# Score bursts across the pairs of a batch, and two PSUM banks left to the MLP

## The chip, the cores and the metric

The kernel runs on one core of a Trainium2 chip. The metric is the device time of one execution in microseconds, as a median of runs. The engines are TensorE (PE, with its weight loads as PEld), VectorE (DVE), ScalarE (ACT), GpSimd (POOL) and SyncE (SP, which here only issues DMAs).

## The reference

Eight batches of eight heads with 576 tokens of 64 dimensions go through causal attention with 16 beacon keys ahead of the keys; the beacons are seen by every query. The result, as 4608 tokens of 512, goes through an MLP with a squared ReLU.

```python
scores = scale * np.matmul(q, k_all.transpose(0, 1, 3, 2))   # k_all: 16 beacons, then 576 keys
scores = np.where(causal, -1000000000.0, scores)
...
a /= a.sum(-1, keepdims=True) + 1e-09
attn = np.matmul(a, v_all)
...
h = x @ w_in            # 4608 x 512 by 512 x 2048
r = np.maximum(h, 0.0)
g = r * r
return (g @ w_out).astype(np.float32)
```

## The kernel before, in words

**Attention.** Work is done by pairs of heads: four pairs a batch, 32 in all, numbered p. Scores are made transposed, with 128 keys on the partitions and the queries along the columns. The two heads of a pair lie in partitions 0 to 63 and 64 to 127 of kT and qT, so that a score matmul (L584) has 64 rows and the two heads' matmuls use the two halves of the PE array. A pair of batches 1 to 7 has four *pieces* (WHOLE): columns 496, 464, 336 + 80 and 208 + 80 of each head. A piece goes into two PSUM banks next to each other, one a head. ScalarE takes its exponential into a tile pt (L597); when all four pieces are there, VectorE sets the causal triangle with a minimum (L607, L611). Then PE makes the product with the values (L627, "av", 30 matmuls of 65 columns, where the 65th column sums the weights), and VectorE divides (L642, L643) into xn. Batches 0 and 1 are transposed for the MLP on PE (L691), the later ones by DMAs from SP's queue. Batch 0 is cut into two phases with pieces of their own (SPLIT).

**MLP.** It goes by nine chunks of 512 tokens. First layer ("s1", L755): for each of 16 blocks of hidden units four matmuls of 512 columns into one bank, then a ReLU on ScalarE (L772) or VectorE (L774), then for each two blocks a squaring on VectorE (L781). Second layer ("s2", L792): for each 128 tokens 16 matmuls into one bank, copied out by ScalarE (L355) and stored.

**The order of the instructions** is planned by the class Order while the kernel is built. Each entry (an Op) has an engine, an estimated duration, a priority (lower goes first), dependencies, and a claim on a pool. Order.run steps through time with these estimates and gives each free engine the ready entry of lowest priority; what it finds is each engine's instruction order on the chip, where semaphores do the waiting. Its rules around the change:

- PSUM is a pool of eight banks (Banks). A request for 2 means an even bank and the next one. Classes have limits on the banks that they may use at once: "strip" (scores) 4, "av" 4, "mlp" 4, "tp" (transposes) 2.
- If a ready entry with a request of more than one part finds no place (`short`), entries of a higher priority number are held to `floors`: the MLP may then not go above 2 banks.
- The score entries of a pair have a `gate` (L555): they wait until the MLP has progressed by a set share for each pair (6.2 us of MLP work). A gated entry is still taken when PE has nothing else.
- Estimates: L310 and L313 for ScalarE and VectorE, LAT (L93) for signals, DRAIN (0.096) on PE for each change between entries of mode "rows" (scores), "columns" and "full".

add_pair claims one of four tiles pt and calls add_phase. There a *burst* is one entry "qk" on PE: all matmuls of two pieces of one pair (of one piece in batch 0), with one claim of 2 banks for each piece. Each piece's exponential is an entry of its own and gives its two banks back. After them add_phase adds the mask, the value product (priority lower than the scores') and the division. All chunks of the MLP have priorities behind every score entry.

Of the kernel before, what the change touches and what calls it, by code (L numbers as in the profile page):

```python
# [88 lines left out]
class Order:  # L89
# [3 lines left out]
    LAT = {"PE": 0.2, "ACT": 0.15, "DVE": 0.12, "POOL": 0.15, "SP": 0.1, "-": 0.0}  # L93
    DRAIN = 0.096

    def __init__(self, pools, limits, floors):
        self.pools = dict(pools)
        self.limits = dict(limits)
        self.floors = dict(floors)
        self.inuse = {k: 0 for k in limits}  # L100
        self.ops = []
        self.progress = 0.0
# [7 lines left out]
    def run(self):  # L110
# [24 lines left out]
        mode = None  # L135
        while events:
            now = events[0][0]
            while events and events[0][0] <= now + 1e-9:
                _, _, kind, op = heapq.heappop(events)
                if kind == "done":  # L140
                    for u in op.users:
                        u.left -= 1
                        if u.left == 0:
                            release(u)
                elif kind == "give":
                    owner, k = op.give if isinstance(op.give, tuple) else (op.give, None)
                    pool, cls, wants = owner.take
                    for i in range(len(wants)) if k is None else [k]:
                        self.pools[pool].give(wants[i], owner.held[i])
                        if cls in self.inuse:  # L150
                            self.inuse[cls] -= wants[i]
            again = True
            while again:
                again = False
                for e in engines:
                    if free[e] > now + 1e-9:
                        continue
                    best = None
                    fallback = None
                    short = min((op.prio for op in avail[e] if op.take and len(op.take[2]) > 1  # L160
                                 and (op.gate is None or op.gate(self))
                                 and self.pools[op.take[0]].find(op.take[2]) is None), default=None)
                    for op in avail[e]:
                        if any(free[x] <= now + 1e-9 for x in op.engs[:op.engs.index(e)]):
                            continue
                        if op.take:
                            pool, cls, wants = op.take
                            if self.pools[pool].find(wants) is None:
                                continue
                            if cls in self.limits:  # L170
                                most = self.limits[cls]
                                if short is not None and op.prio > short:
                                    most = min(most, self.floors.get(cls, most))
                                if self.inuse[cls] + sum(wants) > most:
                                    continue
                        if op.gate is not None and not op.gate(self):
                            if fallback is None or op.prio < fallback.prio:
                                fallback = op
                            continue
                        if op.dma and len(lanes[e]) >= 8 and lanes[e][-8] > now + 1e-9:  # L180
                            continue
                        if best is None or op.prio < best.prio:
                            best = op
                    if best is None:
                        best = fallback
                    if best is None:
                        continue
                    op = best
                    started.add(id(op))
                    for u in op.followers:  # L190
                        u.left -= 1
                        if u.left == 0:
                            release(u)
                    for ee in op.engs:
                        avail[ee].remove(op)
                    if op.take:
                        pool, cls, wants = op.take
                        op.held = self.pools[pool].take(wants)
                        if cls in self.inuse:
                            self.inuse[cls] += sum(wants)  # L200
                    dur = op.dur[e] if isinstance(op.dur, dict) else op.dur
                    if e == "PE":
                        dur += self.DRAIN * (mode not in (None, op.mode))
                        mode = op.mode
                    end = now + dur
                    free[e] = end
                    self.progress += op.pe_time
                    issued.append((op, e, now))
                    seq += 1
                    heapq.heappush(events, (end, seq, "free", op))  # L210
                    if op.dma:
                        dma_free = max(dma_free, now + 0.6) + op.dma
                        seen = max(end, dma_free + 1.6)
                        lanes[e].append(seen)
                        seq += 1
                        heapq.heappush(events, (seen, seq, "free", op))
                    else:
                        seen = end + self.LAT[e]
                    seq += 1
                    heapq.heappush(events, (seen, seq, "done", op))  # L220
                    if op.give is not None:
                        seq += 1
                        heapq.heappush(events, (seen, seq, "give", op))
                    again = True
# [12 lines left out]
def kernel(  # L237
# [11 lines left out]
    nc = tc.nc  # L249
    B, H, S, D = q.shape  # L250
    Nb = beacon_k.shape[2]
    HP = H // 2
# [57 lines left out]
    def act(n):  # L310
        return 0.066 + n / 1200.0
# [6 lines left out]
    def wait_for(later, first):  # L318
# [2 lines left out]

    order = Order(
        pools={"ps": Banks(), "stg": Slots(NSTG), "pt": Slots(NPT)},
        limits={"strip": 4, "av": 4, "mlp": 4, "tp": 2},
        floors={"mlp": 2},
    )
    order.wait_for = wait_for
    add = order.add
# [211 lines left out]
                 (0, 2): 1232, (0, 3): 1360, (1, 2): 1536, (1, 3): 1664, (1, 4): 1792, (0, 4): 1872}),  # L540
    ]
    NSPLIT = 1

    def phases(b):
        return SPLIT if b < NSPLIT else WHOLE

# [4 lines left out]
    def add_pair(b, pr):  # L551
# [11 lines left out]
            qk_deps = trans[b, "k"] + trans[b, "q"]  # L563
        take_pt = add(f"pt{p}", "-", 0.0, None, prio=100.0 * p, deps=qk_deps, take=("pt", "pt", [1]), gate=gate)
        av_ops[p] = []
        for n, ph in enumerate(phases(b)):
            add_phase(b, pr, p, n, ph, take_pt, qk_deps, gate)

    def add_phase(b, pr, p, n, ph, take_pt, qk_deps, gate):
        base = 100.0 * p + 1000.0 * n  # L570
        exps = []
        twos = 2 if b >= NSPLIT else 1
        for i in range(0, len(ph.pieces), twos):
            group = ph.pieces[i:i + twos]
            cols = sum(t1 - t0 for mms, _, _ in group for _, t0, t1, _ in mms)
            box = {}

            def emit_qk(e, group=group, box=box):
                for k, (mms, _, _) in enumerate(group):
                    st = pair(box["qk"], k)  # L580
                    for c, t0, t1, at in mms:
                        for hj in range(2):
                            hp = slice(64 * hj, 64 * hj + 64)
                            nc.tensor.matmul(  # L584
                                st[:, hj, at:at + t1 - t0],
                                kT[b % 2][hp, pr, 128 * c:128 * c + 128],
                                qT[b % 2][hp, pr, t0:t1],
                                start=True, stop=True,
                            )

            qk = add(f"qk{p}.{n}.{i}", "PE", cols / 2400.0, emit_qk, prio=base + i,
                     deps=qk_deps + [take_pt], take=("ps", "strip", [2] * len(group)), gate=gate, mode="rows")
            box["qk"] = qk
            qk_ops[p].append(qk)
            for k, (_, off, width) in enumerate(group):
                def emit_exp(e, off=off, width=width, k=k, box=box):
                    nc.scalar.activation(pt[take_pt.held[0]][:, :, off:off + width],  # L597
                                         pair(box["qk"], k)[:, :, 0:width], AF.Exp, bias=0.0, scale=scale)

                exps.append(add(f"exp{p}.{n}.{i + k}", "ACT", act(2 * width), emit_exp, prio=base + i + k,  # L600
                                deps=[qk], give=(qk, k)))

        def emit_mask(e):
            P = pt[take_pt.held[0]]
            at, step, m0, m = ph.diag
# [226 lines left out]
    for b in range(B):  # L832
# [22 lines left out]
            add_weights()  # L855
        if b == 1:
            add_weights_out()
        for pr in range(HP):
            add_pair(b, pr)
        if b < NXPE:  # L860
            add_xt_pe(b)
        else:
# [41 lines left out]
```

## Time and profile before

| | us |
|---|---|
| median of 3 runs | 348.35 (348.26 to 348.68) |
| the profiled execution | 349.44 |
| its span from first to last instruction | 347.7 |
| PE busy in it | 331.8 |
| ScalarE busy | 202.3 |
| VectorE busy | 150.2 |
| GpSimd busy | 84.8 |

The terms of the prediction are worked out on the profiled execution. A busy time is that in which at least one instruction of the engine was running; matmuls are pipelined, so the length of one row (379 ns for 512 columns) is longer than the distance from one to the next. Rows of the timeline and of the chain have the start, the length, the engine, the tiles and the line, and xN where N instructions in a row are merged. A few per cent of the matmul records are missing: a merged row of the second layer may say x15 where the code has 16.

### The profile page before, as it was taken

To read this page: it belongs to the slowest core of one execution; us is meant where nothing else is said; L and a number is where in the kernel's file an instruction comes from. 1 tells how busy PE (TensorE), PEld (TensorE's weight loads), DVE (VectorE), ACT (ScalarE), POOL (GpSimd) and SP (SyncE) were. 2 spreads that over 40 slices of the span, in tenths; PEclk is the share of its full clock that TensorE was granted. 3 is DMA by queue.
4 is the path that set the end of the run, shared out by engine and by line. 5 is a ranking of instruction groups with operands and counts; after the bars stand their busy time and mean duration, and the time that the engine had idled before them with its cause. 6 is when DMAs were issued, how large, how long until landed. Compare 5 with 4: busy or idle time off the path is not lost.

```text
span 347.7 us, 7270 instructions
## 1 busy us (share of the span) xinstructions
PE 331.8 (95%) x2944; PEld 177.7 (51%) x2980; DVE 150.2 (43%) x306; ACT 202.3 (58%) x311; POOL 84.8 (24%) x132
## 2 busy tenths in 40 slices
PE   3799999999999999999999999999999999999995
PEld 2568765554544444544446874454454444444442
DVE  5466683448722464256523772266323302301300
ACT  2678893497854775577655765677536416614611
POOL 8273740357242046105520452000000000000000
PEclk9999999999999999999999999999999999999999
DMA  7989999899978999899986999750014011011002
GB/s 99 188 126 205 221 206 215 192 248 213 201 150 194 208 207 204 130 237 201 238 173 135 215 242 227 120 139 2 3 60 128 2 60 60 2 60 60 3 15 105
DMA packets 137010, 49.50 MB, mean 142 GB/s; under 512 B 123344, under 2 KB 132048, under 8 KB 136976
## 3 DMA queue, kind: packets, MB, share of 16 engines
q1 hardware_dynamic: 127472, 40.09, 55.7%
q0 software_dynamic: 9504, 8.95, 16.0%
q8 instruction: 23, 0.38, 0.5%
q14 instruction: 11, 0.09, 0.1%
HBM read 37.22 MB, written 9.44 MB: 134 GB/s over the span
## 4 chain that ended last, share of the span: by engine, by line
PE 92%; DMA 3%; issue 2%; ACT 1%; DVE 1%; POOL 0%; SPq 0%; ACTq 0%; POOLq 0%
PE ps L755 36%; PE ps L792 36%; PE ps L627 9%; PE ps L584 8%; DMA stg<-in_v_dram 2%; PE ps L480 1%; DMA qk_area<-in_q_dram 1%; PE ps L691 1%; ACT pt L597 1%; DVE pt L607 1%; PE ps L476 0%; DVE g L774 0%; POOL vb L357 0%; ACT osb L355 0%; POOL qk_area L463 0%
## 5 line engine op out<-in xcount | busy, mean ns | idle before, releaser
L755 PE MATMUL ps<-xT,w_in 128*128 128x512 bf16 (+3 forms) x688 | 132.8, 340 | 1.2 <-issue 0.5
L792 PE MATMUL ps<-w_out,g 128*128 128x512 bf16 x556 | 127.8, 379 | 2.0 <-issue 1.4
L597 ACT ACTIVATE pt<-ps 128x832 bf16<-128x832 f32 (+4 forms) x128 | 103.8, 869 | 43.9 <-PE ps L584 41.9
L755 PEld LDWEIGHTS <-w_in 128*128 128x128 bf16 x704 | 65.1, 98 | 56.1 <-issue 5.3
L772 ACT ACTIVATE g<-ps 128x512 bf16<-128x512 f32 (+2 forms) x128 | 71.7, 560 | 36.0 <-PE ps L755 34.7
L792 PEld LDWEIGHTS <-g 128*128 128x128 bf16 x576 | 53.9, 98 | 66.7 <-issue 4.8
L781 DVE TENSOR_TENSOR g<-g 128x1024 bf16<-128x1024 bf16 (+2 forms) x80 | 51.8, 649 | 71.8 <-ACT g L772 71.0
L355 ACT COPY osb<-ps 128x512 f32<-128x512 f32 x36 | 21.1, 587 | 47.4 <-PE ps L792 41.5
L357 POOL CAST vb<-stg 128x512 bf16<-128x512 f32 (+1 forms) x38 | 26.8, 714 | 78.2 <-DMA stg<-in_v_dram 74.0
L607 DVE TENSOR_TENSOR pt<-pt,tri 128x1024 bf16<-128x1024 bf16 (+1 forms) x36 | 24.8, 693 | 45.4 <-ACT pt L597 44.0
L357 POOL CAST qk_area<-stg 128x512 bf16<-128x512 f32 (+2 forms) x50 | 33.2, 676 | 28.2 <-DMA stg<-in_k_dram 14.8
L627 PEld LDWEIGHTS <-pt 128*128 128x128 bf16 (+1 forms) x960 | 34.9, 100 | 8.6 <-issue 1.6
L627 PE MATMUL ps<-vb,pt 128*128 128x65 bf16 (+1 forms) x960 | 36.8, 197 | 1.0 <-POOL vb L357 0.5
L584 PE MATMUL ps<-qT,kT 64*128 64x80 bf16 (+6 forms) x400 | 36.4, 291 | 1.0 <-ACT pt L597 1.0
L774 DVE TENSOR_SCALAR g<-ps 128x512 bf16<-128x512 f32 (+2 forms) x32 | 19.6, 612 | 19.3 <-PE ps L755 18.9
L643 DVE TENSOR_TENSOR xn<-ps,rcp 128x640 bf16<-128x640 f32 (+2 forms) x36 | 27.0, 751 | 1.3
L584 PEld LDWEIGHTS <-kT 64*128 64x128 bf16 x400 | 13.0, 97 | 21.1 <-issue 17.5
L642 DVE RECIPROCAL rcp<-ps 128x10 f32<-128x10 f32 (+2 forms) x36 | 7.6, 211 | 32.4 <-PE ps L627 32.2
L355 ACT COPY qT<-ps 128x576 bf16<-128x576 bf16 x12 | 7.8, 651 | 11.2 <-PE ps L480 11.2
L480 PE MATMUL ps<-ident,qk_area 96*64 96x96 bf16 x288 | 11.1, 233 | 2.7 <-DMA qk_area<-in_q_dram 1.2
L357 DVE COPY kT<-ps 128x16 bf16<-128x16 bf16 (+1 forms) x24 | 9.9, 453 | 5.2 <-PE ps L480 5.0
L480 PEld LDWEIGHTS <-qk_area 96*64 96x64 bf16 x288 | 8.6, 126 | 4.0 <-DMA qk_area<-in_q_dram 2.1
(31 smaller groups left out, 57.2 us busy)
## 6 DMA issues: line engine op xcount, KB each, us to landing
out_dram<-osb SPq DMA_DIRECT2D x17, 512.0 KB, 3.2
stg<-in_v_dram SPq DMA_DIRECT2D x21, 256.0 KB, 5.7
stg<-in_q_dram SPq DMA_DIRECT2D x20, 256.0 KB, 4.9
stg<-in_k_dram SPq DMA_DIRECT2D x15, 256.0 KB, 5.1
w_in<-in_moe_w_in_dram POOLq DMA_DIRECT2D x4, 512.0 KB, 8.7
w_out<-in_moe_w_out_dram POOLq DMA_DIRECT2D x4, 512.0 KB, 10.9
stg<-in_v_dram SPq DMA_DIRECT2D x7, 224.0 KB, 5.2
qk_area<-in_k_dram POOLq DMA_DIRECT2D x4, 288.0 KB, 12.4
```

Source lines behind the costliest of these rows:

```text
L355: nc.scalar.copy(dst, src)
L357: eng[e].tensor_copy(dst, src)
L480: nc.tensor.transpose(pp[64 * hj:64 * hj + 64, half, at + u * NP:at + (u + 1) * NP], t[b % 2][:, 2 * pr + hj, u, :], ident[0:NP, 0:NP])
L584: nc.tensor.matmul(st[:, hj, at:at + t1 - t0], kT[b % 2][hp, pr, 128 * c:128 * c + 128], qT[b % 2][hp, pr, t0:t1], start=True, stop=True,)
L597: nc.scalar.activation(pt[take_pt.held[0]][:, :, off:off + width], pair(box["qk"], k)[:, :, 0:width], AF.Exp, bias=0.0, scale=scale)
L607: nc.vector.tensor_tensor(out=d, in0=d, in1=tri[:, m0:m0 + m, :][:, None].to_broadcast([128, 2, m, 128]), op=ALU.min)
L627: nc.tensor.matmul(a[:, hj, (t - tl[0]) * (D + 1):(t - tl[0] + 1) * (D + 1)], P[0:rr, hj, o:o + 128], vb[b % 2][0:rr, c, h, :], start=(c = ...
L643: nc.vector.tensor_tensor(out=xn[b % 2].rearrange("p t (h d) -> p h t d", d=D)[:, 2 * pr:2 * pr + 2, tl[0]:tl[0] + nt], in0=a[:, :, :, 0:D ...
L755: nc.tensor.matmul(h[:, lo - spans[0][0]:hi - spans[0][0]], w_in_sb[:, mc, ft * 128:(ft + 1) * 128], xT[:, mc, lo % RING:lo % RING + hi - lo],
L772: nc.scalar.activation(dst, h, AF.Relu, bias=0.0, scale=1.0)
L781: nc.vector.tensor_tensor(out=d, in0=d, in1=d, op=ALU.mult)
L792: nc.tensor.matmul(o, G[:, fc, ts * 128:(ts + 1) * 128], w_out_sb[:, fc, :], start=(fc == 0), stop=(fc == NFT - 1))
```

## The change

Scores are no longer added pair by pair. add_pair now only claims the tile pt and gives a Pair; a new function add_scores lists the pieces of all pairs that it is given and cuts the list into bursts of given sizes. For batch 0 it is called for each pair and phase with bursts of one piece, as before. For batch 1 the sizes are eight times two, so that the bursts are the same pieces as before. For batches 2 to 7 they are 3, 3, 3, 3, 2, 2: pair 0's pieces 0 to 2; its piece 3 with pair 1's 0 and 1; pair 1's 2 and 3 with pair 2's 0; pair 2's 1 to 3; pair 3's 0 and 1; pair 3's 2 and 3. A burst depends on the transposes and tiles of all pairs in it, and has the gate and the priority of its first piece's pair. The limit for "strip" goes from 4 to 6 banks. A new rule, `keep`: once the MLP has begun, an entry of another class may not take banks if fewer would be left than the MLP lacks to two. add_phase keeps the mask, the value product and the division unchanged.

```diff
+                                kept = self.keep - self.inuse["mlp"] if self.progress else 0
+                                if cls != "mlp" and len(self.pools[pool].free) - sum(wants) < kept:
                                     continue
...
-        limits={"strip": 4, "av": 4, "mlp": 4, "tp": 2},
+        limits={"strip": 6, "av": 4, "mlp": 4, "tp": 2},
         floors={"mlp": 2},
+        keep=2,
...
+    SIZES = {b: [2] * 8 if b < 2 else [3, 3, 3, 3, 2, 2] for b in range(B)}
...
-        for n, ph in enumerate(phases(b)):
-            add_phase(b, pr, p, n, ph, take_pt, qk_deps, gate)
+        return Pair(b, pr, p, take_pt, qk_deps, gate)
...
+    def add_scores(pairs, n, sizes):
+
+        work = [(x, i, piece) for x in pairs for i, piece in enumerate(phases(x.b)[n].pieces)]
+        exps = {x.p: [] for x in pairs}
+        at = 0
+        for size in sizes:
+            group = work[at:at + size]
+            at += size
+            prio = 100.0 * group[0][0].p + 1000.0 * n + group[0][1]
...
+            qk = add(f"qk{group[0][0].p}.{n}.{group[0][1]}", "PE", cols / 2400.0, emit_qk, prio=prio,
+                     deps=[d for x in owners for d in x.qk_deps + [x.take_pt]],
+                     take=("ps", "strip", [2] * size), gate=owners[0].gate, mode="rows")
...
+                exps[x.p].append(add(f"exp{x.p}.{n}.{i}", "ACT", act(2 * width), emit_exp, prio=prio + 0.1 * k,
+                                     deps=[qk], give=(qk, k)))
+        assert at == len(work)
+        for x in pairs:
+            add_phase(x.b, x.pr, x.p, n, phases(x.b)[n], x.take_pt, exps[x.p])
...
-        for pr in range(HP):
-            add_pair(b, pr)
+        pairs = [add_pair(b, pr) for pr in range(HP)]
+        if b < NSPLIT:
+            for x in pairs:
+                for n, ph in enumerate(phases(b)):
+                    add_scores([x], n, [1] * len(ph.pieces))
+        else:
+            add_scores(pairs, 0, SIZES[b])
```

More of the change, by code (lines that the diff above doesn't have):

```diff
@@ L94, with __init__ @@
     DRAIN = 0.096
-    def __init__(self, pools, limits, floors):
+    def __init__(self, pools, limits, floors, keep):
+        self.keep = keep
         self.pools = dict(pools)
@@ L174, in run @@
                                 if self.inuse[cls] + sum(wants) > most:
+                                    continue
+                                kept = self.keep - self.inuse["mlp"] if self.progress else 0
+                                if cls != "mlp" and len(self.pools[pool].free) - sum(wants) < kept:
                                     continue
@@ L565, in add_pair, with __init__ @@
         av_ops[p] = []
-        for n, ph in enumerate(phases(b)):
-            add_phase(b, pr, p, n, ph, take_pt, qk_deps, gate)
[L569 to L575, printed above, removed]
+        return Pair(b, pr, p, take_pt, qk_deps, gate)
+    class Pair:
+        def __init__(self, b, pr, p, take_pt, qk_deps, gate):
+            self.b, self.pr, self.p, self.take_pt, self.qk_deps, self.gate = b, pr, p, take_pt, qk_deps, gate
+    def add_scores(pairs, n, sizes):
[6 more added lines that the diff above has]
+            prio = 100.0 * group[0][0].p + 1000.0 * n + group[0][1]
+            cols = sum(t1 - t0 for _, _, (mms, _, _) in group for _, t0, t1, _ in mms)
+            owners = list({x.p: x for x, _, _ in group}.values())
             box = {}
             def emit_qk(e, group=group, box=box):
-                for k, (mms, _, _) in enumerate(group):
+                for k, (x, _, (mms, _, _)) in enumerate(group):
                     st = pair(box["qk"], k)
-                    for c, t0, t1, at in mms:
+                    for c, t0, t1, col in mms:
                         for hj in range(2):
@@ L584, in emit_qk, with emit_exp, add_phase @@
                             nc.tensor.matmul(
-                                st[:, hj, at:at + t1 - t0],
-                                kT[b % 2][hp, pr, 128 * c:128 * c + 128],
-                                qT[b % 2][hp, pr, t0:t1],
+                                st[:, hj, col:col + t1 - t0],
+                                kT[x.b % 2][hp, x.pr, 128 * c:128 * c + 128],
+                                qT[x.b % 2][hp, x.pr, t0:t1],
                                 start=True, stop=True,
                             )
-            qk = add(f"qk{p}.{n}.{i}", "PE", cols / 2400.0, emit_qk, prio=base + i,
-                     deps=qk_deps + [take_pt], take=("ps", "strip", [2] * len(group)), gate=gate, mode="rows")
+            qk = add(f"qk{group[0][0].p}.{n}.{group[0][1]}", "PE", cols / 2400.0, emit_qk, prio=prio,
+                     deps=[d for x in owners for d in x.qk_deps + [x.take_pt]],
+                     take=("ps", "strip", [2] * size), gate=owners[0].gate, mode="rows")
             box["qk"] = qk
[L594 to L597, printed above, removed]
-                                         pair(box["qk"], k)[:, :, 0:width], AF.Exp, bias=0.0, scale=scale)
-                exps.append(add(f"exp{p}.{n}.{i + k}", "ACT", act(2 * width), emit_exp, prio=base + i + k,
-                                deps=[qk], give=(qk, k)))
+            for x in owners:
+                qk_ops[x.p].append(qk)
+            for k, (x, i, (_, off, width)) in enumerate(group):
+                def emit_exp(e, off=off, width=width, k=k, x=x, box=box):
+                    nc.scalar.activation(pt[x.take_pt.held[0]][:, :, off:off + width],
+                                         pair(box["qk"], k)[:, :, 0:width], AF.Exp, bias=0.0, scale=scale)
+                exps[x.p].append(add(f"exp{x.p}.{n}.{i}", "ACT", act(2 * width), emit_exp, prio=prio + 0.1 * k,
[3 more added lines that the diff above has]
+            add_phase(x.b, x.pr, x.p, n, phases(x.b)[n], x.take_pt, exps[x.p])
+    def add_phase(b, pr, p, n, ph, take_pt, exps):
+        base = 100.0 * p + 1000.0 * n
         def emit_mask(e):
```

## The prediction

> **What bounds the kernel now.** I read the page first, its engine shares and its slices.
>
> ```profile
> span 347.7 us, 7270 instructions
> PE 331.8 (95%) x2944; PEld 177.7 (51%) x2980; DVE 150.2 (43%) x306; ACT 202.3 (58%) x311; POOL 84.8 (24%) x132
> PE   3799999999999999999999999999999999999995
> PEclk9999999999999999999999999999999999999999
> PE 92%; DMA 3%; issue 2%; ACT 1%; DVE 1%; POOL 0%; SPq 0%; ACTq 0%; POOLq 0%
> ```
>
> PE is busy from the third slice to the last, at full clock, and carries 92% of the chain that ended last. A busy PE is not proof of a dense one, so the waits of PE come next.
>
> ```profile
> PE ps L476 <- DVE bks L448: 4.2, 1, 4.2
> ...
> PE ps L584 <- ACT pt L597: 1.0, 2, 0.8
> PE ps L627 <- POOL vb L357: 0.5, 1, 0.5
> ...
> PE ps L627 <- DVE pt L607: 0.4, 1, 0.4
> ```
>
> The largest wait lies in the start, at 4 us. What PE waits for ScalarE's exponentials is 1.0 us in two waits, for a mask 0.4 us, and for an MLP bank nothing. From about 26 us, where the MLP begins, the time is therefore the sum of what PE issues. So the question is how long each kind of PE work takes from its start to the next start. That is read in the timeline of PE in a middle stretch (start, length, line, shapes, count).
>
> ```profile
> 159.35 0.58 PE L584 MATMUL ps<-qT,kT 64*128 64x496 bf16 x4
> 159.86 2.76 PE L755 MATMUL ps<-xT,w_in 128*128 128x512 bf16 x12
> 162.56 0.48 PE L584 MATMUL ps<-qT,kT 64*128 64x336 bf16 x8
> 162.97 3.63 PE L755 MATMUL ps<-xT,w_in 128*128 128x512 bf16 x16
> 166.43 1.09 PE L627 MATMUL ps<-vb,pt 128*128 128x65 bf16 x30
> ```
>
> The starts count here, since lengths overlap. From 162.97 to 166.43 are 3.46 us for 16 matmuls of 512 columns: 0.216 us each, 0.42 ns a column, with nothing lost before the value product (L627). Score matmuls stand out. The two heads of a pair use 64 rows each and run side by side, so a burst's columns count once. Pieces 0 and 1 have 496 + 464 = 960 columns, 0.40 us at that pace, but from 159.35 to 159.86 are 0.51. Pieces 2 and 3 have 416 + 288 = 704, 0.30 us, but from 162.56 to 162.97 are 0.41. Each leaves 0.11 us behind the burst. In front, 12 matmuls from 159.86 should end 2.59 us later, and the burst starts 2.70 later: 0.11 us again, rounded from starts of 10 ns, so I take 0.10. **A burst costs its columns and about 0.21 us for going into the 64-row form and back**, whatever its number of matmuls (4 and 8 alike).
>
> **The sum, part by part.** *Fewer bursts.* Before, each pair of batches 2 to 7 has two bursts: 6 x 4 x 2 = 48. After, a batch has six: 36. The same columns are streamed, so what goes is 12 x 0.21 = 2.5 us of PE time. On PE nothing hides it, since PE is the path. No instruction is added on any engine: exponentials, masks and products keep shapes and counts, and no DMA is issued more or less.
>
> The Trainium skill, TensorEngine Tiling (Array Packing), section Key Properties, says that changing the tiling mode drains the array; the trace agrees, with the 0.10 and 0.11 us above. The Trainium skill, TensorE: Matmul & The Clock Gate, section Phases on the wall clock, gives a drain about 128 cycles, 53 ns at 2.4 GHz; 24 switches at that figure would give an estimate of 1.3 us in place of 2.5, and the measured duration is used.
>
> *What late exponentials and fewer free banks cost.* A burst of three takes six of the eight PSUM banks, and the MLP has two until the first exponential has freed a pair. This state is not in the trace as such, so I bound it. The rows are those of what must pass through ScalarE and VectorE, with shapes kept apart.
>
> ```profile
> L755 PE MATMUL ps<-xT,w_in 128*128 128x512 bf16 x432 | 101.2, 379 | 1.2 <-issue 0.5
> L772 ACT ACTIVATE g<-ps 128x512 bf16<-128x512 f32 x105 | 62.8, 598 | 33.8 <-PE ps L755 33.3
> L781 DVE TENSOR_TENSOR g<-g 128x1024 bf16<-128x1024 bf16 x64 | 44.7, 700 | 67.2 <-ACT g L772 66.4
> L597 ACT ACTIVATE pt<-ps 128x832 bf16<-128x832 f32 x36 | 31.0, 867 | 16.4 <-PE ps L584 14.4 <-issue 1.4 <-DVE rcp L642 0.4
> L597 ACT ACTIVATE pt<-ps 128x928 bf16<-128x928 f32 x32 | 30.5, 953 | 0.0
> L597 ACT ACTIVATE pt<-ps 128x992 bf16<-128x992 f32 x28 | 28.0, 1001 | 26.2 <-PE ps L584 26.2
> L607 DVE TENSOR_TENSOR pt<-pt,tri 128x1024 bf16<-128x1024 bf16 x28 | 21.7, 773 | 42.3 <-ACT pt L597 42.2
> L774 DVE TENSOR_SCALAR g<-ps 128x512 bf16<-128x512 f32 x23 | 15.9, 690 | 18.3 <-PE ps L755 17.9
> ```
>
> One MLP bank is held for three matmuls' spacing and the last one's 379 ns, 0.65 + 0.38 = 1.03 us, then for a ReLU of 0.60 on ScalarE or 0.69 on VectorE, and two signals of about 0.05 us. That is 1.73 to 1.82 us, where two banks in turn allow 2 x 0.863 = 1.73. So with two banks the first layer just keeps pace if each ReLU starts at once. If it finds ScalarE in an exponential (0.87 to 1.00 us) and VectorE in a squaring or mask (0.70 or 0.77), PE waits for the rest of the shorter one.
>
> How long does this state last? A burst's three exponentials take 1.00 + 0.95 + 0.87 = 2.8 us. The second burst of a batch has the first pair as its first owner and so the same gate; it stands ready at once, finds no three free pairs, and while that is so the planner holds the MLP to its floor of two banks. So one stretch of about 3 us in each batch is throttled; bursts three and four wait for their gates, and are throttled only while banks drain. In the second layer nothing of this matters: there a bank is held for 16 matmuls, 3.46 us, so two are ample. How loaded the evacuating engines are shows in the windows of a first-layer and a second-layer stretch.
>
> ```profile
> core 0: us, PE busy (x) PEld busy (x) DVE busy (x) ACT busy (x) POOL busy (x), PEclk, DMA share, GB/s
> 114.00:132.40 18.40, 18.29 (x156) 8.81 (x158) 11.32 (x20) 14.51 (x22) 5.67 (x8) 1.00 1.07 214
> 132.40:152.00 19.60, 19.28 (x165) 9.39 (x166) 5.31 (x12) 10.39 (x15) 4.91 (x8) 1.00 0.97 162
> ```
>
> In the first layer ScalarE is busy 14.51 of 18.40 us and VectorE 11.32, in the second 10.39 and 5.31 of 19.60. A chunk of 512 tokens has 64 matmuls in each layer, so about half of the 24 bursts of three fall on the first layer, 12. Bounds for what PE loses at one of them: nothing (before, PE loses nothing to MLP banks although strips and a value product leave it two there also), and 0.77 us, a mask or squaring that has just begun. In sum 0 to 9.2 us. I take 0.08 us a burst, **0.9 us**, near the lower end, because the planner fills such a place with a value product (0.9 us) where it has one, and because ReLUs go ahead of exponentials in its order; its costs are short by some 0.1 us of a ReLU, which is why it is not nothing.
>
> *The strip limit of six* also holds in batches 0 and 1, where sizes do not change. The two waits of a score burst for ScalarE, 1.0 us, lie there; a third strip in flight lets PE issue earlier, but ScalarE still works its exponentials off in the same time. Bounds: 1.0 us gained, and 0.5 us lost if a value product comes to wait like the 0.5 us row for L627. I take **0.3 us gained**.
>
> *The kept banks* cost instructions nothing. They can hold back a value product or a score burst until the MLP holds two banks; the lead of attention covers that. The chain shows it for batch 2.
>
> ```profile
> 93.38 1.03 PE ps L627 x30
> ...
> 114.47 1.62 PE ps L755 x7
> ```
>
> Batch 2's last value product ends at 94.4 us (its fourth in the chain, behind four of batch 1), and the MLP's chunk that needs it starts at 114.5: 20 us of cover. The same cover hides that a pair's fourth piece now comes with the next pair's first two, some 3 us later, and that its mask, product and the transposes through SP's queue follow as late. If the cover were gone, those 3 us would show once a batch.
>
> *The end* does not move: after the last burst PE runs 85 us of MLP alone, with nothing changed.
>
> Sum: -2.5 + 0.9 - 0.3 = **-1.9 us**. The profiled execution took 349.44 us (span 347.7, 1.7 outside it), 1.1 above the median of the runs; the terms are PE time that both have. Forecast: 348.35 - 1.9 = 346.4 us, own range 345.6 to 347.5.
>
> **The rivals.** *All is gained.* The planner finds a value product or a free bank for every place, and the 1.0 us of the start goes too: -2.5 - 1.0 = -3.5, 344.9 us. For it speaks that PE waits for no MLP bank now; against it the 3 us stretch with two banks and no slack.
>
> *Given back.* The waits take what the switches gave, 0.2 us at each of the 12 bursts: about 348.3 us. For it speaks that 1.82 us for a ReLU on VectorE is over the 1.73 that two banks allow, 0.05 us a bank turn and some four turns a stretch, before any queueing.
>
> *Slower: the MLP on two banks waits behind exponentials.* Place: the first-layer matmuls (L755) that follow a burst of three. Price: a ReLU comes at a random point of VectorE's 0.70 to 0.77 us while ScalarE is in its exponentials, so half of one, about 0.4 us, at 12 bursts: 4.8 us, less 2.5: 2.3 slower, 350.6 us. It decides from 0.21 us a burst on. For it speaks ScalarE's 79% in such stretches; against it that before shows 0 there, with VectorE at 62%. The Trainium skill, TensorEngine Tiling (Array Packing), section PSUM Bottleneck, warns of this: faster matmuls leave the emptying of PSUM as the bound. The trace of before does not show it.
>
> That the bursts are not formed can be left out: one planner entry emits all pieces of a burst in one go.
>
> **How the numbers follow.** Forecast 0.50, all gained 0.13, given back 0.16, slower 0.21. About 0.2% (0.7 us) is what a measurement of this kernel can tell from no change; 347.65 and 349.05 are those bounds. Faster: the first two, less 0.01 of the forecast's upper end, 0.62. Same: 0.17. Slower: 0.21. The range, 345.0 to 350.0 us, leaves out half of the best case and half of the slow one, which reaches further up as a wait may cost 0.77.
>
> **What would show it right or wrong.** The timeline of PE should have 12 or 16 matmuls of L584 in a burst with six bursts a batch, each with about 0.21 us above its columns. The waits of PE should still name nearly nothing for L755; if they name ACT L597, ACT L772 or DVE L774 with over 2.5 us in all, the slow rival is right. If the start of L755 at 26 us moves by more than 1 us, the strip limit in batches 0 and 1 was mis-sized. The forecast is wrong too if a burst of three costs more than its columns and 0.21 us.

## The result, and the profile after

The changed kernel takes 346.25 us in the median of 20 runs, the kernel before 348.65, or 2.4 us less. The ratio, which leaves out the one execution of 351.1 us as a slow one, is 0.9945, with an interval of 0.9926 to 0.9964; it stands for 1.9 us. The times of after spread more: 345.5 to 351.1 us, where those of before lie between 348.1 and 349.4. The profiled execution took 346.09 us.

The page of after, in the lines that answer to those of before:

```profile
span 344.4 us, 7251 instructions
PE 329.1 (96%) x2940; PEld 178.1 (52%) x2980; DVE 154.3 (45%) x304; ACT 200.2 (58%) x313; POOL 84.6 (25%) x132
PE 81%; DMA 8%; SPq 4%; POOL 3%; issue 2%; ACT 0%; DVE 0%; POOLq 0%; DVEq 0%; ACTq 0%
```

PE is still the bound, but no longer alone: of the chain that ended last, 15% now run over DMAs, SyncE's queue and GpSimd, where it was some 3% before. The waits of PE say where (L597 is the score matmul now, L612 the exponential, L775 the first layer, L812 the second, L647 the value product, L694 the issue of the tokens' DMA transposes):

```profile
PE ps L485 <- DMA qk_area<-in_k_dram: 1.4, 1, 1.4
PE ps L775 <- DMA xT<-xn: 1.2, 1, 1.2
PE ps L647 <- POOL vb L362: 0.7, 2, 0.4
...
PE ps L597 <- ACT pt L612: 0.6, 1, 0.6
```

The second row is new: the first layer waits once for transposed tokens. No row names ScalarE or VectorE for an MLP bank. In the timeline of PE, two bursts of three and, as the last, one across two pairs look like this:

```profile
91.43 1.89 PE L812 MATMUL ps<-w_out,g 128*128 128x512 bf16 x8
93.25 0.76 PE L597 MATMUL ps<-qT,kT 64*128 64x496 bf16 x8
...
190.00 0.76 PE L597 MATMUL ps<-qT,kT 64*128 64x496 bf16 x8
190.69 3.74 PE L775 MATMUL ps<-xT,w_in 128*128 128x256 bf16 x32
194.35 0.70 PE L597 MATMUL ps<-qT,kT 64*128 64x208 bf16 x8
194.99 2.79 PE L775 MATMUL ps<-xT,w_in 128*128 128x256 bf16 x24
```

From 190.00 to 190.69 are 0.69 us for 496 + 464 + 416 = 1376 columns, which are 0.57 us: 0.12 behind the burst. The one at 194.35 has 288 + 960 = 1248 columns, 0.52 us, in 0.64: 0.12 again. In front, eight matmuls of 0.216 us from 91.43 should end at 93.16, and the burst starts at 93.25: 0.09. So three pieces pay for the change of form the 0.21 us that two paid. These bursts have 8 matmuls, others 10, since a piece has two or four; the prediction's 12 or 16 were miscounted, but its sum does not use them.

Where was the wait for tokens prepared? The chain of after, followed back from it (start, length, what):

```profile
94.90 6.05 DMA stg<-in_k_dram
...
101.00 0.62 POOL qk_area L362
101.63 0.32 SPq L406
...
102.00 0.42 SPq L407
...
102.47 0.02 SPq L694
...
106.39 2.50 DMA xT<-xn
...
109.03 1.02 PE ps L775 x4
```

A load of batch 4's keys lands at 100.95, GpSimd's cast frees its staging tile, and SyncE issues the next loads. Only then come the five token transposes of batch 2, which stand behind them in its queue. The same stretch of SyncE's queue in both kernels, before first:

```profile
90.85 4.49 SPq L402 DMA_DIRECT2D stg<-in_q_dram  x4
95.43 2.01 SPq L402 DMA_DIRECT2D stg<-in_k_dram  x1
97.56 7.32 SPq L674 DMA_TRANSPOSE xT<-xn  x5
```

```profile
97.30 3.71 SPq L407 DMA_DIRECT2D stg<-in_k_dram  x3
...
102.00 0.42 SPq L407 DMA_DIRECT2D stg<-in_v_dram  x1
102.51 6.44 SPq L694 DMA_TRANSPOSE xT<-xn  x5
```

The transposes go out 5 us later (102.5 in place of 97.6), and their last is through at 108.95 in place of 104.88. And the MLP wants them earlier. PE's timeline around the start of chunk 2's first layer, before and then after:

```profile
114.40 1.90 PE L755 MATMUL ps<-xT,w_in 128*128 128x512 bf16 x8
```

```profile
105.88 1.90 PE L812 MATMUL ps<-w_out,g 128*128 128x512 bf16 x8
109.03 1.02 PE L775 MATMUL ps<-xT,w_in 128*128 128x512 bf16 x4 [1.25 <-DMA xT<-xn]
```

In after, eight matmuls of 0.216 us from 105.88 end at 107.6, and PE would go on with chunk 2; before it was there at 114.4.

### The profile page after: what moved, and what is told of

Read it like the earlier page. It is cut to its first block, busy times and chain, and to the rows that moved or that the text cites. A ratio compares the mean times of both kernels' runs of the same rounds, so it can differ in the third digit from the quotient of the medians.

```text
span 344.4 us, 7251 instructions
## 1 busy us (share of the span) xinstructions
PE 329.1 (96%) x2940; PEld 178.1 (52%) x2980; DVE 154.3 (45%) x304; ACT 200.2 (58%) x313; POOL 84.6 (25%) x132
## 4 chain that ended last, share of the span: by engine, by line
PE 81%; DMA 8%; SPq 4%; POOL 3%; issue 2%; ACT 0%; DVE 0%; POOLq 0%; DVEq 0%; ACTq 0%
PE ps L775 33%; PE ps L812 32%; PE ps L647 8%; PE ps L597 7%; DMA stg<-in_q_dram 2%; DMA stg<-in_v_dram 2%; POOL qk_area L362 2%; DMA stg<-in_k_dram 2%; SPq L407 1%; PE ps L485 1%; SPq L439 1%; SPq L694 1%; POOL vb L362 1%; DMA qk_area<-in_q_dram 1%; PE ps L711 1%
## 5 line engine op out<-in xcount | busy, mean ns | idle before, releaser
L775 PE MATMUL ps<-xT,w_in 128*128 128x512 bf16 (+3 forms) x686 | 132.8, 339 | 2.2 <-DMA xT<-xn 1.2
L812 PE MATMUL ps<-w_out,g 128*128 128x512 bf16 x554 | 128.2, 379 | 1.5 <-issue 0.5
L612 ACT ACTIVATE pt<-ps 128x832 bf16<-128x832 f32 (+4 forms) x128 | 102.8, 870 | 17.3 <-PE ps L597 17.2
L775 PEld LDWEIGHTS <-w_in 128*128 128x128 bf16 x704 | 65.4, 98 | 57.6 <-issue 8.2
L792 ACT ACTIVATE g<-ps 128x512 bf16<-128x512 f32 (+2 forms) x127 | 70.5, 555 | 39.7 <-PE ps L775 38.4
L801 DVE TENSOR_TENSOR g<-g 128x1024 bf16<-128x1024 bf16 (+2 forms) x80 | 54.4, 683 | 80.5 <-ACT g L792 78.7
L812 PEld LDWEIGHTS <-g 128*128 128x128 bf16 x576 | 53.8, 98 | 63.6 <-issue 2.9
L360 ACT COPY osb<-ps 128x512 f32<-128x512 f32 x36 | 21.2, 590 | 67.0 <-PE ps L812 64.5
L362 POOL CAST vb<-stg 128x512 bf16<-128x512 f32 (+1 forms) x38 | 25.0, 668 | 84.8 <-DMA stg<-in_v_dram 83.6
L362 POOL CAST qk_area<-stg 128x512 bf16<-128x512 f32 (+2 forms) x50 | 34.5, 702 | 36.2 <-DMA stg<-in_k_dram 26.3
L647 PEld LDWEIGHTS <-pt 128*128 128x128 bf16 (+1 forms) x960 | 34.6, 99 | 7.1 <-issue 1.8
L647 PE MATMUL ps<-vb,pt 128*128 128x65 bf16 (+1 forms) x960 | 36.1, 196 | 0.7 <-POOL vb L362 0.7
L597 PE MATMUL ps<-qT,kT 64*128 64x80 bf16 (+7 forms) x400 | 34.3, 294 | 0.7 <-ACT pt L612 0.6
L794 DVE TENSOR_SCALAR g<-ps 128x512 bf16<-128x512 f32 (+2 forms) x33 | 21.0, 639 | 15.0 <-PE ps L775 14.7
L597 PEld LDWEIGHTS <-kT 64*128 64x128 bf16 x400 | 14.0, 99 | 20.9 <-issue 16.4
L360 ACT COPY qT<-ps 128x576 bf16<-128x576 bf16 x12 | 7.8, 650 | 11.8 <-PE ps L485 11.8
L631 DVE TENSOR_TENSOR pt<-pt,tri 80x160 bf16<-80x160 bf16 x32 | 10.7, 333 | 0.0
```

Source lines behind the costliest of these rows:

```text
L360: nc.scalar.copy(dst, src)
L362: eng[e].tensor_copy(dst, src)
L597: nc.tensor.matmul(st[:, hj, col:col + t1 - t0], kT[x.b % 2][hp, x.pr, 128 * c:128 * c + 128], qT[x.b % 2][hp, x.pr, t0:t1], start=True, s ...
L612: nc.scalar.activation(pt[x.take_pt.held[0]][:, :, off:off + width], pair(box["qk"], k)[:, :, 0:width], AF.Exp, bias=0.0, scale=scale)
L647: nc.tensor.matmul(a[:, hj, (t - tl[0]) * (D + 1):(t - tl[0] + 1) * (D + 1)], P[0:rr, hj, o:o + 128], vb[b % 2][0:rr, c, h, :], start=(c = ...
L775: nc.tensor.matmul(h[:, lo - spans[0][0]:hi - spans[0][0]], w_in_sb[:, mc, ft * 128:(ft + 1) * 128], xT[:, mc, lo % RING:lo % RING + hi - lo],
```

## The experiments

Theory after the result: three terms. The strip limit of six gains about 1.9 us in batch 0 (far more than the 0.3 that I had taken), 12 bursts fewer gain up to 2.5 us, and a wait for a DMA, in a place that hangs on the order of SyncE's queue, takes part of it back. Rivals: the gain is all in the bursts; or the loss is in the MLP's two banks. All ratios are to the kernel before on the same chip.

**The strip limit alone.**

```diff
-        limits={"strip": 4, "av": 4, "mlp": 4, "tp": 2},
+        limits={"strip": 6, "av": 4, "mlp": 4, "tp": 2},
```

> The kernel before with one number changed: the limit for strips 6 in place of 4; bursts stay two pieces of one pair, no kept banks. Theory (start): the third strip in batch 0 lets about 1.9 us of score and value products run ahead of the MLP's first matmul (counted in the two traces: three bursts of 0.39 us and 24 matmuls of the value product, 0.7 us, that stood behind it before), so 1.9 us faster than before, about 346.7 us. Rival (the prediction's own term): 0.3 us faster, 348.3 us. Rival (only the number of bursts matters): the same as before within 0.2 us.

Measured: 346.96 us, ratio 0.9949 (0.9935 to 0.9964), 1.9 us less. So one number alone gives as much as three quarters of the result. What moved shows in the matmuls of the scores (first line) and of the value product (second) up to 25.8 us, about where the MLP starts; for the kernel before

```profile
4.00:25.80 21.80, 5.94 (x56) 2.61 (x56) 1.00 0.95 154
4.00:25.80 21.80, 4.69 (x72) 4.20 (x72) 1.00 0.95 154
```

and for this one (PE busy and count, the weight loads, then the granted clock):

```profile
4.00:25.80 21.80, 6.21 (x64) 2.75 (x64) 0.92 0.97 154
4.00:25.80 21.80, 4.36 (x96) 3.75 (x96) 0.92 0.97 154
```

The counts are the reading: eight score matmuls (two bursts of 0.38 us) and 24 of the value product (0.7 us) more run in PE's idle time, by estimate 1.5 of the 1.9 us. The busy times do not compare, since the granted clock was 0.92 here. In after, at 1.00, the same 64 and 96 matmuls are busy for 6.78 and 5.09 us, 1.24 us more than in before. That the gain lies in batches 0 and 1 is for the next run to show, as the limit holds in all batches.

**The other way round: the changed kernel with the old limit for batches 0 and 1.**

```diff
-        limits={"strip": 6, "av": 4, "mlp": 4, "tp": 2},
+        limits={"strip": 6, "strip0": 4, "av": 4, "mlp": 4, "tp": 2},
-                     take=("ps", "strip", [2] * size), gate=owners[0].gate, mode="rows")
+                     take=("ps", "strip" if pairs[0].b >= 2 else "strip0", [2] * size), gate=owners[0].gate, mode="rows")
```

> The changed kernel with the old strip limit of 4 for batches 0 and 1 alone. Theory (start): 1.9 us slower than after, about 348.1 us, with the first MLP matmul at the same 26 us but three bursts and a value product more behind it. Rival (the start gains 0.3 us): 346.6 us.

Measured: 348.76 us, ratio 0.9995 (0.9975 to 1.0015): slower than after by 2.5 us in the medians and 1.7 in the ratios, on the side of the theory of the start and not of its rival. So without the start, bursts of three and kept banks together gain nothing here. In its profile PE waits 1.5 us for xT, as after does for 1.2. That is not all of the 2.5 us that its fewer switches should give, and the rest stays open (its times go from 347.2 up to 353.7).

**Bursts of two everywhere in the changed code, and in batch 2 alone.**

```diff
-    SIZES = {b: [2] * 8 if b < 2 else [3, 3, 3, 3, 2, 2] for b in range(B)}
+    SIZES = {b: [2] * 8 for b in range(B)}                                    # run twos
+    SIZES = {b: [2] * 8 if b < 3 else [3, 3, 3, 3, 2, 2] for b in range(B)}   # run batch2_twos
```

> The changed kernel with bursts of two pieces in batches 2 to 7 as well (48 bursts there in place of 36); strip limit 6 and kept banks stay. Theory (start plus switches plus a wait for the transposed tokens): the 2.5 us of 12 switches come back, the start's 1.9 us stay, and the wait of the first-layer matmuls for the tokens' transposes (1.2 us in the profile of after) is gone: 1.9 us faster than before, about 346.7, and hardly slower than after; the times spread by about 1 us as those of before, not by 5 us as those of after. Rival (the gain is all in the bursts): as before, 348.5 us, 2.3 us slower than after.

> The changed kernel with bursts of two in batch 2 alone; batches 3 to 7 keep 3, 3, 3, 3, 2, 2. Theory: after loses its wait and its spread in batch 2 only, where pairs finish out of order and the tokens' transposes stand behind loads in SyncE's queue; here 10 of the 12 switches stay away (2.1 us), the start's 1.9 us stay, the wait goes: 4.0 us faster than before, about 344.6 us, times within about 1.2 us of each other. Rival (the spread comes from bursts of three everywhere, by the MLP on two banks): 0.4 us slower than after, 346.6 us, and times still spread over 5 us.

Measured: 349.14 us, ratio 1.0015 (1.0001 to 1.0028), and 349.04 us, ratio 0.9997 (0.9982 to 1.0013). Both miss the theory, by 2.4 and 4.4 us. twos comes near its rival's time, but not for the rival's reason, and batch2_twos misses its rival too. The wait for tokens is gone from both, but PE now waits for keys, 3.4 us in twos and 3.9 in batch2_twos. For twos, the wait of PE, then its timeline, then SyncE's queue:

```profile
PE ps L597 <- DMA kT<-qk_area: 3.4, 3, 2.2
```

```profile
122.28 3.62 PE L775 MATMUL ps<-xT,w_in 128*128 128x512 bf16 x16
128.06 0.58 PE L597 MATMUL ps<-qT,kT 64*128 64x496 bf16 x4 [2.16 <-DMA kT<-qk_area]
```

```profile
90.65 7.25 SPq L694 DMA_TRANSPOSE xT<-xn  x5
97.95 1.20 SPq L407 DMA_DIRECT2D stg<-in_v_dram  x2
...
121.37 4.96 SPq L439 DMA_TRANSPOSE kT<-qk_area  x1
```

Here the planner put the token transposes first. SyncE stands from 89.5 to 90.7 for them and issues them until 97.9. The loads behind come 10 to 11 us later than in after (the first at 97.95 against 87.78), so that batch 4's keys are transposed at 121.4 in place of 114.5. The wait has changed its object: keys in place of tokens. So I changed the theory: what takes the gain back is the order of one queue between two users, each of which binds PE when it comes second.

**That order alone, in the kernel of twos.**

```diff
         load_chain.append(ld)
+        if (b, x, c) == (4, "k", 4):
+            for t2 in range(NT):
+                xt_ops[2, t2].behind.append(ld)
```

> The kernel of run twos (bursts of two everywhere, strip limit 6, kept banks) with one place in SyncE's queue changed: the five transposes of batch 2's tokens are issued behind batch 4's last key load, in place of ahead of batch 3's last two value loads. Theory (order of SyncE's queue): twos was slow because the queue stood for those tokens, so that batch 4's loads, casts and key transpose came 10 us later and PE waited 2.3 us and twice 0.6 us for keys; with the loads first the waits go: 349.1 - 2.2 = 346.9 us, as the kernel before with strip limit 6. Rival (the new burst code or the kept banks cost this time by themselves): 349.1 us again.

Measured: 346.95 us, ratio 0.9943 (0.9926 to 0.9959): 2.2 us less than twos, with the same bursts and with 0.2 us of waiting for kT in all. The queue's order is the cause of those 2.2 us; the new code and the kept banks cost nothing with bursts of two (346.95 against 346.96 of the strip limit alone).

**The price of a change of form, by itself.** In the kernel before:

```diff
                     st = pair(box["qk"], k)
+                    if k and b >= 2:
+                        nc.tensor.matmul(st[:, 0, 500:501], ident[:, :], ident[:, 0:1], start=True, stop=True)
```

> The kernel before with one full-array matmul of one column between the two pieces of each score burst of batches 2 to 7 (48 in all; it writes a column of PSUM that nothing reads): each burst now goes into the 64-row form twice. Theory: 48 x (0.21 us for the switches + 0.03 us for the matmul) = 11.5 us slower, 360.2 us. Rival (a drain of 53 ns a switch): 48 x (0.11 + 0.03) = 6.7 us slower, 355.4. Rival (the price hangs on the burst's other neighbours, not on the switch): 1.4 us slower, 350.1.

Measured: 358.88 us, ratio 1.0293 (1.0270 to 1.0315), 10.1 us more: 0.21 us for each of the 48, the small matmul included, or 0.18 if that takes the 0.03 expected of it. The theory's 11.5 lies just above the interval of 9.4 to 11.0. The drain of 53 ns a switch, with 6.7 us, is excluded, and so is the rival with 1.4. In PE's timeline, 0.28 us from the last score matmuls' start (336 + 80 columns are 0.17) and 0.11 behind the one column:

```profile
157.49 0.35 PE L586 MATMUL ps<-qT,kT 64*128 64x336 bf16 x4
157.77 0.18 PE L582 MATMUL ps<-ident 128*128 128x1 bf16 x1
157.88 0.30 PE L586 MATMUL ps<-qT,kT 64*128 64x208 bf16 x4
```

**Without the kept banks.**

```diff
-        keep=2,
+        keep=0,
```

> The changed kernel without the kept banks (keep 0), all else the same. Theory: strips with six banks and a value product with two can then hold all eight, the MLP has none until the first exponential (1.0 us) or the division (1.05 us) gives a pair back, and PE has nothing else: about 0.6 us at one place in each of the six batches, 3 to 4 us slower than after, 349.5 to 350.5 us, with the order planned so that PE stands before L775 or L812. Rival (the rule does nothing, since the floor of two does the same): 346.3 us.

Measured: 355.36 us, ratio 1.0152 (1.0111 to 1.0193): 9 us slower than after in the medians and 7 in the ratios, about twice what was expected. The waits show two parts:

```profile
PE ps L775 <- ACT osb L360: 3.9, 1, 3.9
PE ps L775 <- DVE xn L663: 3.5, 5, 1.0
```

The five waits for the division (3.5 us) are the expected ones: with strips and a value product on all eight banks, the MLP has none. The single one of 3.9 us was not. Its chain:

```profile
219.94 1.25 SPq L694
...
221.29 3.97 DMA out_dram<-osb
...
225.36 0.59 ACT osb L360
```

The eviction of an output tile (L360) waited for the store of an earlier one, which went out at 221.3 behind five token transposes in SyncE's queue and landed 4 us later. What follows it is told at the end. So of the 9 us only the five waits belong to the kept banks by what the profile shows; their 3.5 us alone are more than the 2.5 that bursts of three save. The rest is SyncE's queue a third time: 3.9 us of waiting and, by the estimate at the end, 1.7 us at a lower clock. Whether without that wait the loss would be 5 us, as the lowest of its four times (351.94) suggests, was not tried.

**Versions that spare both users of the queue.** Run keeplate takes bursts of two in batch 2 and begins the kept banks later:

```diff
-                                kept = self.keep - self.inuse["mlp"] if self.progress else 0
+                                kept = self.keep - self.inuse["mlp"] if self.progress > 27.7 * 1.5 else 0
```

> The changed kernel with bursts of two in batch 2 (as in run batch2_twos) and with the rule of the kept banks from 1.5 chunks of MLP work on, which leaves SyncE's queue up to batch 4 in the order of the kernel before. Theory (sum): start -1.9, 10 switches -2.1, no wait for tokens or keys: 4.0 us faster than before, 344.5 us, with times within about 1.5 us. Rival (bursts of three lose to two MLP banks or to keys in batches 3 to 7): 346 us or more, with L775 waiting for ACT or DVE, or L597 for kT.

Measured: 346.80 us, ratio 0.9936 (0.9917 to 0.9955), a miss by 2.3 us, with the rival's mark: PE ps L597 waits 1.1 us for kT in its profile. Two ways to give those keys more time, and after once more on the same chip:

```diff
-    LEAD, PACE = -0.4, 0.225
+    LEAD, PACE = -0.3, 0.225                          # run lead3, on top of keeplate
...
+        if (b, x, c) == (4, "k", 4): ...              # run keys_first: the edit of twos_4k4, on top of keeplate
```

> The kernel of run keeplate with the gates of all score bursts 0.1 of a chunk later (LEAD -0.3 in place of -0.4): batch 4's first burst comes some 3 us later against its keys. Theory (keys): keeplate lost 1.1 us in its profile, and more in other executions, to PE waiting for kT; with 3 us more the wait goes: 346.8 - 1.5 = 345.3 us, with less spread. Rival (keeplate's lost 2 us are bank waits of the bursts of three): 346.8 us again.

> The kernel of run keeplate with the five transposes of batch 2's tokens behind batch 4's last key load in SyncE's queue, as in run twos_4k4. Theory (keys): batch 4's key transpose comes about 4 us earlier, the wait for kT goes, and the tokens still come before chunk 2 wants them: 345.3 us. If the tokens are late instead, L775 waits for xT and the time is 346.5 or more. Rival (bank waits): 346.8 us again.

> The changed kernel once more, to be compared on one chip with the other two and to give a second profile. Theory: its times spread over more than 3 us, and the wait of L775 for xT is there again with another length; outside it the profile is that of after.

Measured: lead3 345.40 us, ratio 0.9902 (0.9887 to 0.9917), five times between 344.85 and 345.89; keys_first 345.95 us, 0.9913 (0.9898 to 0.9928), five times between 344.84 and 346.19 and one of 350.35; after again 346.42 us, 0.9935 (0.9912 to 0.9958), from 345.01 to 349.74. In lead3's waits nothing of tokens or keys is left; after the first loads of the start, the largest are

```profile
PE ps L597 <- ACT pt L612: 0.6, 1, 0.6
PE ps L647 <- POOL vb L362: 0.4, 1, 0.4
```

It is the fastest kernel here, though not apart from keys_first, and 1.0 us under after on one chip, with two bursts more. Its interval and after's just overlap, but its times are close together. After's second profile has the same wait again, 1.1 us for xT.

The profile of keys_first is that of its 350.35 us. It has no wait for tokens or keys, but the one of nokeep, with the kept banks in place: PE waits for the eviction of an output tile (L360), and ScalarE for the store of an earlier one. That store went out at 216.25 behind five token transposes and landed 5.2 us later. In after, too, ScalarE waits for a store behind five transposes, too shortly for PE to wait. PE's row in keys_first, then ScalarE's in after:

```profile
PE ps L778 <- ACT osb L360: 3.1, 1, 3.1
```

```profile
ACT osb L360 <- DMA out_dram<-osb: 1.3, 1, 1.3
```

The profiles of start4 (1.8 us), of after again (0.8), of nokeep (5.7) and of keys_first itself (4.9) have that row of ScalarE's as well, those of the other kernels do not. In lead3's profile that store stands ahead of the transposes (207.75 against 208.38).

**The bursts of three, once no DMA is late.** lead3 with bursts of two everywhere:

```diff
-    SIZES = {b: [2] * 8 if b < 3 else [3, 3, 3, 3, 2, 2] for b in range(B)}
+    SIZES = {b: [2] * 8 for b in range(B)}
```

> The kernel of run lead3 with bursts of two in batches 3 to 7 as well, nothing else changed: 10 bursts more, and SyncE's queue is in the same order up to batch 4, so that neither tokens nor keys are late in either kernel. Theory (a switch is worth 0.21 us a burst once no DMA wait takes it back): 10 x 0.21 = 2.1 us slower than lead3, 347.5 us. Rival (bursts of three lose part of it to banks): less than 1 us slower, 346.4 us or below.

Measured: 347.13 us, ratio 0.9949 (0.9935 to 0.9963). Between 0.9902 and 0.9949 lie 1.6 us for ten bursts, 0.16 each: nearer to the theory's 2.1 than to the rival's 1 or less. The two intervals together allow 0.9 to 2.4 us, so that the times alone do not exclude the rival. Its sign is nearly absent: in lead3's profile PE waits 0.2 us for a ReLU of VectorE (PE ps L775 <- DVE g L794) and for no other bank of the first layer.

## Why the prediction was right, and which of its steps failed

*Fewer bursts, -2.5 us.* The mechanism and, nearly, the price held: 0.18 to 0.21 us by toggle, 0.16 by lead3 and lead3_twos. For 12 bursts that is 1.9 to 2.5 us. The Trainium skill, TensorEngine Tiling (Array Packing), section Key Properties, says that a change of mode drains the array, and the runs agree; the estimate of 1.3 us from the drain in TensorE: Matmul & The Clock Gate (the Trainium skill, section Phases on the wall clock) was too low by half.

*The strip limit in batches 0 and 1, -0.3 us.* Mis-sized: -1.9 us, outside my bounds of -1.0 to +0.5. I had bounded it by the waits of PE that the profile puts down to the exponentials (1.0 us). But a limit in the planner also shapes the order of the instructions. Much of PE's idle time in the start comes between instructions that wait for other things, and what a looser order fills into them isn't bounded by the row of one releaser. Nor did the sign that I had named for it show: the first matmul of the MLP started at 25.90 us before and at 25.81 after, with more work ahead of it.

*The MLP on two banks, +0.9 us.* It did not come: no wait for a bank in the profile of after, with bursts of three beside the first layer, as above. That holds with the kept banks; without them PE does wait for banks, though for the division's and not, as I had it, for the ReLU's (3.5 us in nokeep). I had said of that rule that it costs instructions nothing and is covered, but not that it keeps this loss away.

*The cover of 20 us.* This step failed. I had read it from the end of the last value product to the first layer that wants its tokens. Between them lies SyncE's in-order queue, in which the five transposes took 7.3 us (97.56 to 104.88 before) and may stand behind loads, so that the cover was not 20 but 9.5 us (from 104.9 to 114.4). The change spent it from both sides: PE reached chunk 2 6.8 us sooner (107.6), with less attention done ahead of it (294 matmuls of the value product since the MLP's start, in place of 348), and the tokens came 4.1 us later (108.95). That is 1.4 us more than the cover, and PE's timeline shows a wait of 1.25. Part of the delay is that pairs finish out of order: batch 2's last division ends at 97.95 us in after and at 95.55 in before. The timeline of after shows the bursts of batch 2; that those of two go first because they find room sooner is my reading of the planner:

```profile
75.03 0.70 PE L597 MATMUL ps<-qT,kT 64*128 64x208 bf16 x8
...
77.50 0.58 PE L597 MATMUL ps<-qT,kT 64*128 64x496 bf16 x4
...
80.77 0.48 PE L597 MATMUL ps<-qT,kT 64*128 64x336 bf16 x8
...
83.02 0.69 PE L597 MATMUL ps<-qT,kT 64*128 64x336 bf16 x10
...
89.95 0.67 PE L597 MATMUL ps<-qT,kT 64*128 64x464 bf16 x10
```

The two bursts of pair 3 (77.50 and 80.77) go ahead of those of pairs 1 and 2 (83.02 and 89.95). I had looked at each DMA's count and not at its place in the queue.

The sum came out by luck, because the errors cancel: -1.9 of the start in place of -0.3, no bank waits in place of +0.9, and a wait of 1.2 us in the profile, which I had not named. -2.5 - 1.9 + 1.2 = -3.2 is near the difference of the two profiled spans, 347.7 - 344.4 = 3.3. But before's profiled execution was 0.8 us above its median, and the medians differ by 2.4. With 1.9 to 2.5 us for the bursts, what after loses again is then, by estimate, 1.4 to 2.0 us.

Where the wider spread of after comes from is not shown. The wait for tokens is 1.2 and 1.1 us in its two profiles, so hardly different. The store behind the transposes is the likelier source: ScalarE's wait for it goes from 0.8 to 5.7 us in the five profiles that have it, PE waited 3.1 and 3.9 us in the two longest, and the times of these five runs spread over 3.6 to 6.5 us, those of the others over 0.8 to 3.0. But no run moved that store alone.

## What to carry to other kernels

When an engine that sets the time gets faster, ask which in-order queue feeds it and how long its oldest transfer has until it is wanted. Read that from the landing of the last DMA, not from the end of the work that starts it. In a planned order, one change of a limit or a size moves the issues on every queue, so that a part which looks slow by itself (twos, 2.2 us) may only have drawn a bad order; put the order right before judging the part. And try the smallest number in a change by itself: here one limit alone gave 1.9 of 2.4 us.

## What the runs showed of the hardware

In nokeep, PE stood nearly idle for 4 us, and then its granted clock was low. The windows (busy times, then PEclk):

```profile
222.00:226.00 4.00, 0.05 (x2) 0.00 (x1) 0.00 (x0) 0.64 (x2) 0.00 (x0) 1.00 0.82 238
226.00:230.00 4.00, 4.00 (x14) 1.61 (x14) 0.84 (x2) 1.74 (x3) 0.61 (x1) 0.66 0.18 68
230.00:234.00 4.00, 3.47 (x45) 2.28 (x45) 1.49 (x3) 2.84 (x4) 0.00 (x0) 0.92 0.42 146
```

The clock is 0.66 in the 4 us after the wait and 0.92 in the next: by estimate a single wait of 4 us costs about 1.7 us more afterwards (0.34 x 4 + 0.08 x 4). In keys_first PE stood idle for 3.1 us, until 222.2, with the same sequel:

```profile
222.00:226.00 4.00, 3.79 (x11) 1.38 (x11) 0.84 (x2) 2.06 (x4) 0.61 (x1) 0.61 0.90 258
```

The wait of 1.2 us in after leaves the clock at full (1.00 from 109 to 112 us). The Trainium skill, TensorE: Matmul & The Clock Gate, section HAM oscillation — how this bites in real kernels, warns of idle gaps over about 3.4 us; nokeep's trace agrees with its 3.9, and keys_first's shows it at 3.1 too.
